# A fused attention and feed-forward kernel: the start planned on given landing times, V of batch 1 loaded last, stores later in their queue

## The chip, the cores and the metric

The kernel runs on one core of one Trainium2 chip. The time is the device time of one execution in microseconds (us). The engines are named as in the profile: PE (TensorE, matrix multiplication), PEld (its weight loads), DVE (VectorE), ACT (ScalarE), POOL (GpSimd) and SP (SyncE, which here only issues DMAs).

## The reference

Attention over a window of 64 positions for 8 batches, 8 heads, 576 positions and a head size of 64, then a feed-forward layer with a hard-swish on the 4608 x 512 result:

```
scores = q @ k.T / sqrt(64), kept where 0 <= i - j < 64
attn   = softmax(scores);  x = attn @ v          # x: 4608 x 512
h = x @ w_in                                     # 4608 x 2048
out = (h * clip(h + 3, 0, 6) / 6) @ w_out        # 4608 x 512
```

All inputs and the output are float32. The kernel computes in bfloat16 with float32 sums.

## The kernel before, in words

**Tiles.** The feed-forward layer runs over nine tiles `t` of 512 tokens. A tile has a first part of 16 groups `fc` of four 512-column matmuls with `win` (line L600), whose results pass through ACT (L613) and DVE (L618) into `gT`, and a second part of 64 matmuls with `wout` (L637) into four output blocks `u`, each copied to `osb` (L648) and stored by SP. A batch has 576 tokens, so a tile holds the rows of one or two batches; attention of batch `t + 1` is worked into tile `t`. Attention goes by pairs of heads `g` (0 to 3). The last 64 positions of all pairs form one extra item, "e".

**Attention of a pair.** `scores` (L444) multiplies 64-row blocks of K and Q, ACT takes the exponential (L460). For batch 0 a mask called `far` is added by two matmuls beforehand (L437); later batches multiply by `mask` on DVE (L469). The product with V has two forms. `pv` (L541) gives the transposed result and, through columns of ones in `V`, the sums; ACT takes their logarithm and an exponential (L547, L550) and DVE multiplies (L561) into `xT`. `pv_rows` (L489) gives rows and sums in one, DVE divides (L499, L500), and `turn_x` (L515) transposes the result on PE, to be copied to `xT` (L297). Batch 0's pairs take the second form, all others the first.

**How Q and K come in transposed.** For batches 0 and 1 POOL loads them with a cast into `Aq` and `Ak`, and PE transposes them by `fold_pair` (18 small matmuls, L409; copied out at L414). From batch 2 on SP loads float32 rows into a `stage` buffer, POOL casts them to `nq` and `nk` (L297), and SP transposes by DMA (`turn`, L320), first Q, then K. V is always loaded by SP into a stage and cast into `V` (`cast_v`, L297).

**What sets the order.** Each operation is added to a `Plan` with its engine, an estimated duration, what it reads and writes, a priority and sometimes operations that it must follow. `settle` runs through the plan with estimated times eight times and emits all instructions in the order of their planned start. So a number in the plan issues nothing itself, but it moves instructions on every engine's queue, and the engines run their queues in order. A DMA's planned end comes from `landing`, a model of the two DMA queues (SP's and POOL's). POOL's DMAs and some of its other work are tied in a chain by `then`: in batch 0's stage q and k of pairs 1 to 3, the masks, `touch` (a one-column copy that reads a loaded buffer, so that what follows waits for that load; before, it reads V of pair 2), the four parts of `win`, the first two of `wout`, q and k of batch 1, the last two of `wout`, and `hold`. `hold` writes into the stage buffer of batch 1's V, so V's loads on SP wait for it. Before, it is a memset; the plan lists `wout` part 2 as what it reads, but the instruction itself reads nothing.

**Filling matmuls.** Ahead of the first tile `warm` (L805) puts matmuls with `ident` into planned gaps of PE, sized by the gap.

Of the kernel before, what the change touches and what calls it, by code (L numbers as in the profile page):

```python
# [10 lines left out]
F32 = mybir.dt.float32  # L11
# [10 lines left out]
WINDOW = 64  # L22
FAR = 8.0e9


class Op:
    def __init__(self, eng, dur, emit, reads, writes, prio, stream):
# [9 lines left out]
        self.packets = self.cost = 0  # L37
# [4 lines left out]
class Plan:  # L42
# [4 lines left out]
    LAT = 150  # L47
    NSLOT = {"n": 2, "b": 1, "a": 2}
# [37 lines left out]
    def landing(self, begin, packets, cost, other):  # L86
        now, left = begin, packets
        for a, b, c in other:
# [6 lines left out]
            per = 0.9 * (cost + c) / 16  # L95
# [6 lines left out]
    def solve(self, rank, seen):  # L102
# [4 lines left out]
        free = {}  # L107
# [8 lines left out]
        while left:  # L116
            best = None
            for key, lst in streams.items():
                cands = lst[:1] if key in inorder else lst[:24]
                for op in cands:  # L120
# [51 lines left out]
            if op.packets:  # L172
# [3 lines left out]
                op.done = ring[eng] + 700  # L176
# [12 lines left out]
def kernel(  # L189
# [9 lines left out]
    nc = tc.nc  # L199
# [58 lines left out]
    HEAD = 2  # L258
    LATE = 13
# [55 lines left out]
    def dma(packets, cost, out_ap, in_ap, reads=(), writes=(), stream="ld", after=(), kind="copy", eng="SP"):  # L315
# [5 lines left out]
        op = add(eng, 760 if eng == "POOL" else 480, em, reads=reads, writes=writes,  # L321
# [14 lines left out]
    def load_pair(n, src, b, g, i, x):  # L336
        st = stage[i][:, x * R * D : (x + 1) * R * D]
        dma(P, 106, st, src[b, 2 * g : 2 * g + 2].rearrange("h (p j) d -> (h p) (j d)", j=R), writes=[("stp", n)])
        copy_op(R * D, A[n][:, g, :, :].rearrange("p j d -> p (j d)"), st, ("ACT", "DVE"),
                [("stp", n)], [("A", n, g)] + st_keys(i, 0, NG, range(KB)), sbuf=True, prio=700)  # L340
# [6 lines left out]
    def load_tok(src, b, i, g0, g1, kbs=tuple(range(KB))):  # L347
        st = stage[i][:].rearrange("p (k h d) -> p k h d", k=KB, h=H)
        hs = slice(2 * g0, 2 * g1)
        for kb in kbs:  # L350
# [3 lines left out]
                writes=[("st", i, g, kb) for g in range(g0, g1)])  # L354

    def st_keys(i, g0, g1, kbs):
        return [("st", i, g, kb) for g in range(g0, g1) for kb in kbs]
# [17 lines left out]
    def v_keys(g):  # L375
        return ["V1"] + [("V", g, x) for x in (0, NE + 1, NE + 2)]
# [21 lines left out]
    def fold_pair(n, g, b, gate, kinds=("n", "b", "a")):  # L398
# [3 lines left out]
        op = pe(R * 30, None, [("A", n, g), "fold"], [key], "pick", alloc=(name,), kinds=kinds, after=gate, mode="r")  # L402
# [19 lines left out]
    def scores(b, items, gate, stream="att", pr=300, masked=False, kinds=("a",)):  # L422
# [5 lines left out]
        op = pe(sum(2 * (NG if e else NM) * 14 for e in ends) + (2 * mm(MAIN) if masked else 0), None,  # L428
# [49 lines left out]
    def pv_rows(b, g, i, after, stream="att", pr=300):  # L478
# [4 lines left out]
        op = pe(2 * NM * 17, None, [("pT", i)] + v_keys(g), [key], stream, alloc=(name,), kinds=("a", "b"), after=after, mode="c")  # L483
# [208 lines left out]
    scrap = sb([P, 1], F32, "scrap")  # L692

    def touch(i, g, kb, after=()):

        st = stage[i][:].rearrange("p (k h d) -> p k h d", k=KB, h=H)
        return add("POOL", 100, lambda: nc.gpsimd.tensor_copy(out=scrap[:], in_=st[:, kb, 2 * g, 0:1]),
# [150 lines left out]
```

## Time and profile before

| | before |
|---|---|
| runs shown, us | 310.7, 311.97, 313.28; median 311.97 |
| profiled execution, us | 310.29, span 308.6 |
| granted TensorE clock | 1.000 |
| PE busy | 296.0 us (96%) |
| PEld / DVE / ACT / POOL busy | 51% / 63% / 69% / 28% |
| moved by DMA | 48.18 MB, 156 GB/s over the span |

The page gives the busy time of each engine, the chain of work that ended last, and the groups of instructions. A row of the timeline has the start, the time, the engine, the line, the operation with `out<-in` and the count of instructions merged, and in brackets the idle time of the engine before it and what ended it. SPq is SP's queue of DMA issues. In an answer on DMAs, the last number of an issue's row is the median time from issue to landing.

### The profile page before, as it was taken

The page shows a single profiled execution, that of the slowest core. Times are in us where ns is not written, and L with a number is a line of the kernel's source. Part 1 is how long each engine was busy: PE and PEld are TensorE (multiplying, and loading weights), DVE is VectorE, ACT ScalarE, POOL GpSimd, SP SyncE. Part 2 cuts the span into 40 slices and gives each one's busy share as a digit, 9 for nine tenths or more (in the row PEclk, how much of TensorE's full clock was granted, in tenths as well). Part 3 has the DMA queues.
Part 4 walks back from the last instruction along what each step waited for, and adds up shares of the span by engine and source line. Part 5 has one row for each costly group of instructions (what it writes and reads, how often), then busy time and mean ns, then how long its engine had stood idle before and what let it go on. Part 6 is the DMA issues. An engine that isn't in the chain of part 4 may idle for free.

```text
span 308.6 us, 6865 instructions
## 1 busy us (share of the span) xinstructions
PE 296.0 (96%) x2777; PEld 157.2 (51%) x2777; DVE 193.0 (63%) x292; ACT 213.2 (69%) x332; POOL 87.0 (28%) x82
## 2 busy tenths in 40 slices
PE   4989999899899999999999999999999999999995
PEld 3774455443554455445588654455445544444442
DVE  4366767876497758476857685797577757206700
ACT  3748967785697878687868795879587957217611
POOL 7683003333643345433445000683400000000000
PEclk9999999999999999999999999999999999999999
DMA  8999995999999999999999999939100110010011
GB/s 184 170 205 192 199 212 161 225 213 241 214 221 209 259 208 185 235 278 202 203 177 224 244 208 211 240 20 220 71 0 12 58 71 0 34 71 34 0 68 68
DMA packets 136703, 48.18 MB, mean 156 GB/s; under 512 B 125920, under 2 KB 131808, under 8 KB 136672
## 3 DMA queue, kind: packets, MB, share of 16 engines
q1 hardware_dynamic: 130496, 41.50, 64.3%
q0 software_dynamic: 6176, 6.26, 12.4%
q8 instruction: 21, 0.34, 0.5%
q14 instruction: 10, 0.08, 0.1%
HBM read 36.70 MB, written 9.44 MB: 150 GB/s over the span
## 4 chain that ended last, share of the span: by engine, by line
PE 72%; issue 2%; DMA 2%; DVE 1%; ACT 1%
PE pn L637 34%; PE pn L600 13%; PE pa L600 10%; PE pb L600 8%; PE pa L541 3%; DMA Tk<-nk 2%; PE pa L444 2%; DVE xT L561 1%; PE pb L541 1%; PE pb L444 1%; ACT rec L547 0%; ACT osb L648 0%; ACT rec L550 0%
## 5 line engine op out<-in xcount | busy, mean ns | idle before, releaser
L637 PE MATMUL pn<-wout,gT 128*128 128x512 bf16 x576 | 132.1, 379 | 0.1
L600 PEld LDWEIGHTS <-win 128*128 128x128 bf16 x640 | 61.9, 98 | 62.0 <-issue 2.0
L637 PEld LDWEIGHTS <-gT 128*128 128x128 bf16 x576 | 53.7, 98 | 59.5 <-issue 0.4
L600 PE MATMUL pn<-xT,win 128*128 128x512 bf16 (+1 forms) x284 | 65.0, 358 | 0.0
L297 POOL CAST V<-stage 64x2048 bf16<-64x2048 f32 (+2 forms) x22 | 39.2, 1784 | 52.1 <-DMA stage<-in_v_dram 22.8
L613 ACT ACTIVATE t<-pn,half 128x512 bf16<-128x512 f32 x64 | 44.1, 689 | 8.9 <-PE pn L600 7.6
L600 PE MATMUL pa<-xT,win 128*128 128x512 bf16 (+1 forms) x208 | 48.6, 358 | 1.2 <-DVE xT L561 1.2
L618 DVE SCALAR_TENSOR_TENSOR gT<-t,pn 128x512 bf16<-128x512 bf16 x64 | 43.9, 686 | 9.3 <-ACT t L613 9.0
L618 DVE SCALAR_TENSOR_TENSOR gT<-t,pa 128x512 bf16<-128x512 bf16 x47 | 32.2, 687 | 22.8 <-ACT t L613 22.5
L561 DVE TENSOR_TENSOR xT<-pa,rec 64x512 bf16<-64x512 f32 (+1 forms) x52 | 34.8, 668 | 12.5 <-ACT rec L550 11.5
L613 ACT ACTIVATE t<-pa,half 128x512 bf16<-128x512 f32 x47 | 32.2, 686 | 9.7 <-PE pa L600 9.2
L648 ACT COPY osb<-pn 128x512 f32<-128x512 f32 x23 | 13.4, 582 | 35.7 <-PE pn L637 35.7
L618 DVE SCALAR_TENSOR_TENSOR gT<-t,pb 128x512 bf16<-128x512 bf16 x33 | 22.6, 686 | 23.5 <-ACT t L613 23.5
L600 PE MATMUL pb<-xT,win 128*128 128x512 bf16 (+1 forms) x148 | 34.8, 356 | 0.0
L547 ACT ACTIVATE rec<-pa 64x512 f32<-64x512 f32 (+1 forms) x52 | 29.9, 575 | 2.9 <-PE pa L541 1.0
L297 POOL CAST nq<-stage 128x2048 bf16<-128x2048 f32 (+1 forms) x12 | 15.6, 1319 | 56.3 <-DMA Tq<-nq 28.3
L613 ACT ACTIVATE t<-pb,half 128x512 bf16<-128x512 f32 x33 | 22.8, 690 | 8.5 <-PE pb L600 8.5
L460 ACT ACTIVATE pT<-pa 128x1024 bf16<-128x1024 f32 x25 | 24.5, 1021 | 5.4 <-PE pa L444 5.4
L469 DVE TENSOR_TENSOR pT<-pT,mask 128x1024 bf16<-128x1024 bf16 x28 | 22.1, 809 | 8.0 <-ACT pT L460 7.9
L541 PEld LDWEIGHTS <-V 128*128 128x128 bf16 x512 | 18.8, 98 | 6.9 <-DVE xT L561 0.7
L550 ACT ACTIVATE rec<-rec 128x512 f32<-128x512 f32 (+1 forms) x36 | 20.8, 577 | 0.7
L297 POOL CAST nk<-stage 128x2048 bf16<-128x2048 f32 (+1 forms) x12 | 14.9, 1267 | 14.9 <-DMA stage<-in_k_dram 14.0
(80 smaller groups left out, 174.6 us busy)
## 6 DMA issues: line engine op xcount, KB each, us to landing
out_dram<-osb SPq DMA_DIRECT2D x36, 256.0 KB, 2.4
stage<-in_q_dram SPq DMA_DIRECT2D x24, 256.0 KB, 4.7
stage<-in_k_dram SPq DMA_DIRECT2D x24, 256.0 KB, 5.2
stage<-in_v_dram SPq DMA_DIRECT2D x24, 256.0 KB, 5.2
stage<-in_v_dram SPq DMA_DIRECT2D x22, 128.0 KB, 6.2
win<-in_moe_w_in_dram POOLq DMA_DIRECT2D x4, 512.0 KB, 8.4
wout<-in_moe_w_out_dram POOLq DMA_DIRECT2D x4, 512.0 KB, 16.8
stage<-in_q_dram SPq DMA_DIRECT2D x6, 128.0 KB, 4.8
```

What stands on the lines that cost most here:

```text
L297: alts = {e: (cost[e], (lambda e=e: cpy(e)(out=out_ap, in_=src())), sbuf) for e in engines}
L460: nc.scalar.activation(out=p_[:].rearrange("p j h c -> p h j c"), in_=wide(op, name)[:, :, 0 : n * D].rearrange("p h (j c) -> p h j c", c= ...
L469: nc.vector.tensor_tensor(out=pp, in0=pp, in1=mask[:, m0 : m0 + n, :, :].rearrange("p j h c -> p (j h c)"), op=MULT)
L541: nc.tensor.matmul(wide(op, name)[:, h, y * D : (y + 1) * D], lhsT=V[:, blk, g, h * D : h * D + P], rhs=p_[:, y, h, :], start=True, stop=True)
L547: add("ACT", act(n), lambda h=h: nc.scalar.activation(out=rc[rows[h], 0:n], in_=wide(op, name)[rows[1 - h], h, 0:n], func=LN), reads=[key] ...
L550: add("ACT", act(n), lambda: nc.scalar.activation(out=rc[:, 0:n], in_=rc[:, 0:n], func=EXP, scale=-1.0), writes=[("rc", ri, 0), ("rc", ri, ...
L561: nc.vector.tensor_tensor(out=o, in0=a, in1=z, op=MULT)
L600: nc.tensor.matmul(bank(op, name)[:, to : to + n], lhsT=win16[:, g, fc * P : (fc + 1) * P], rhs=xT[:, g, o : o + n], start=(g == 0), stop= ...
L613: nc.scalar.activation(out=t1[ti][:], in_=bank(op, name), func=RELU, bias=half[:], scale=1.0 / 6.0)
L618: nc.vector.scalar_tensor_tensor(out=gT[:, fc, :], in0=t1[ti][:], scalar=1.0, in1=bank(op, name), op0=MIN, op1=MULT)
L637: nc.tensor.matmul(bank(op, name), lhsT=gT[:, fc, col : col + P], rhs=wout16[:, fc, :], start=(fc == 0), stop=(fc == NFC - 1))
L648: alts = {e: (f(DM), (lambda e=e: cpy(e)(out=osb[oi][:], in_=bank(op, name))), False) for e, f in (("DVE", dve), ("ACT", act))}
```

## The change

In the plan: the first 18 loads get landing times from a table, stores may not be planned earlier than 3 us after their result is ready, a DMA transpose is planned with 4.6 us of SP's time, and some costs differ. In the program:

- Batch 0: q and k of pair 2 are issued ahead of the masks and those of pair 3 behind them; `mask` (used from the end item of batch 0 on) is built later. `touch` reads `Aq` of pair 3, so `win` waits for that load. V of pairs 2 and 3 is cast pair by pair.
- Of the columns of ones in `V`, DVE writes the two that batch 0's pairs need, and POOL the rest, ahead of `hold`.
- `wout` and batch 1 by turns: two parts, q and k of pairs 0 and 1, two parts, q and k of pairs 2 and 3. `hold` is a copy that reads the last part of `wout`.
- Batch 1's pairs 1, 2 and 3 take `pv_rows` and `turn_x`.
- Filling matmuls have 256 columns instead of 128 and fill 0.6 of a gap instead of 0.8.

In the order that comes of it, PE takes the scores of batch 2's pairs 0 and 1 ahead of the first 12 matmuls of `wout` of the second tile instead of behind them; on SP the ten loads of batch 1's V stand without a store between them, two stores stand between the transposes of batch 2 where a store, two loads of V and one of q stood, and the last two loads of batch 2's V stand behind both transposes.

```diff
+LANDED = {
+    "SP": (2950, 3650, 6000, 6700, 7500, 8300, 11100, 11600, 12100, 13200, 13500, 13700),
+    "POOL": (4500, 6300, 7800, 9000, 10000, 10900),
+}
...
+    LAG = 3000
...
-            per = 0.9 * (cost + c) / 16
+            per = (1.1 if 79 in (cost, c) else 0.9) * (cost + c) / 16
...
+                            if op.stream == "st":
+                                t = max(t, d.done + self.LAG)
...
-                op.done = ring[eng] + 700
+                op.done = max(op.land or ring[eng] + 600, t + dur)
+                ring[eng] = max(ring[eng], op.done - 600)
...
+    HOLD = 3
+    ROWS = (1, 2, 3)
...
-        op = add(eng, 760 if eng == "POOL" else 480, em, reads=reads, writes=writes,
+        op = add(eng, 740 if eng == "POOL" else 4600 if kind == "turn" else 500, em, reads=reads, writes=writes,
...
-    def attend(b, first, second, stream="att"):
+    def attend(b, first, second, stream="att", rows=()):
...
-            pv(b, x, i, (), stream)
+            if x in rows:
+                _, *og = pv_rows(b, x, i, (), stream)
+                turn_x(b, x, *og, stream, kinds=("b", "a"))
+            else:
+                pv(b, x, i, (), stream)
...
-    def touch(i, g, kb, after=()):
+    def touch(n, g, after=()):
...
+        return add("POOL", 200, lambda: nc.gpsimd.tensor_copy(out=scrap[:], in_=A[n][:, g, 0, 0:1]),
+                   reads=[("A", n, g)], writes=["scrap"], after=after, prio=2000)
...
-    def hold(i, reads, after=()):
+    def hold(i, part, after=()):
...
-        return add("POOL", 80, lambda: nc.gpsimd.memset(stage[i][:, 0:1], 0.0), reads=reads,
-                   writes=st_keys(i, 0, NG, range(KB)), after=after)
+        return add("POOL", 200, lambda: nc.gpsimd.tensor_copy(out=stage[i][:, 0:1], in_=wout16[:, 4 * part + 3, 0:1]),
+                   reads=[("wout", part)], writes=st_keys(i, 0, NG, range(KB)), after=after)
...
+    then(load_cast("q", q, 0, 2, 3, after=chain))
+    then(load_cast("k", k, 0, 2, 3, after=chain))
+    then(add("POOL", 1050, mask_pool, writes=["m32"], after=chain))
+    then(add("POOL", 900, far_pool, reads=["m32"], writes=["far"], after=chain))
+    then(load_cast("q", q, 0, 3, 4, after=chain))
+    then(load_cast("k", k, 0, 3, 4, after=chain))
...
-    first = cast_v(iv, 0, 2, (THREE,) * 3, prio=700)
-    then(touch(iv, 2, 0, chain))
+    cast_v(iv, 0, 2, (("POOL", "DVE"),) * 3, prio=700)
+    then(touch("q", NG - 1, chain))
...
     for g in range(0, NG, 2):
+        for i in range(2):
+            then(load_wout(g + i, after=chain))
+        if g == 0:
+            then(add("POOL", 1300, mask_pool16, reads=["m32"], writes=["mask"], after=chain))
         then(load_cast("q", q, 1, g, g + 2, after=chain))
         then(load_cast("k", k, 1, g, g + 2, after=chain))
-    for i in range(2, 4):
-        then(load_wout(i, after=chain))
...
-    then(hold(iv, [("wout", 2)], chain))
+    then(add("POOL", 1900, lambda: nc.gpsimd.memset(V[:, :, :, D + 2 : 2 * D], 1.0), writes=["V2"], after=chain))
+    then(hold(iv, HOLD, chain))
...
-    rank = {("PE", "att"): 300, ("PE", "pick"): 300, ("POOL", "issue"): 300, ("SP", "turn"): 1000, ("SP", "st"): 500}
+    rank = {("PE", "att"): 300, ("PE", "pick"): 300, ("POOL", "issue"): 0, ("SP", "turn"): 1000, ("SP", "st"): 500}
```

More of the change, by code (lines that the diff above doesn't have):

```diff
@@ L36, in __init__ @@
         self.got = {}
-        self.packets = self.cost = 0
+        self.packets = self.cost = self.land = 0
         self.home = eng
@@ L811 @@
                 if at is not None and at < COLD:
-                    for _ in range(int((op.start - at) * 0.8 / mm(P))):
+                    for _ in range(int((op.start - at) * 0.6 / mm(2 * P))):
                         warm(op)
```

67 lines of the change are left out of this document (33 added, 34 removed).

## The prediction

> **What bounds the kernel now.** I read the page first, then the busy time by windows, then the timeline of the first 97 us, then the DMA answers of single windows.
>
> ```profile
> span 308.6 us, 6865 instructions
> ...
> PE 296.0 (96%) x2777; PEld 157.2 (51%) x2777; DVE 193.0 (63%) x292; ACT 213.2 (69%) x332; POOL 87.0 (28%) x82
> ...
> 120.00:150.00 30.00, 30.00 (x254) 14.83 (x253) 20.50 (x32) 23.00 (x38) 10.57 (x7) 1.00 1.15 224
> ...
> 119.47 5.18 PE pn L637 x24
> ```
>
> The second number of a window row is the TensorE busy time, the third from the end the granted clock, full here. Between 120 and 150 us, in the third and fourth tile, TensorE is busy in every microsecond, and the row of the chain gives 5.18/24 = 0.216 us for one 512-column matmul; nothing in this change makes that cheaper. All that can be won lies before about 95 us: in the start, and in the waits of the first two tiles. The timeline of the start (start, duration, engine, line, operation, idle time before it):
>
> ```profile
> 4.36 0.69 POOL L318 DMA_DIRECT2D Aq<-in_q_dram  x1
> 5.68 0.69 PE L409 MATMUL pn<-fold,Aq 64*64 64x64 bf16 x18
> 6.69 0.89 POOL L683 TENSOR_SCALAR far<-mask 128x64 bf16<-128x64 f32 x2
> 8.89 2.72 SPq L318 DMA_DIRECT2D stage<-in_v_dram  x1
> 8.98 0.47 PE L409 MATMUL pa<-fold,Aq 64*64 64x64 bf16 x18
> 11.32 1.02 ACT L460 ACTIVATE pT<-pb 128x1024 bf16<-128x1024 f32 x1 [0.24 <-PE pb L444]
> 12.94 1.54 POOL L318 DMA_DIRECT2D win<-in_moe_w_in_dram  x2 [0.28 <-issue]
> 13.55 0.76 DVE L414 COPY Tq<-pn 128x576 bf16<-128x576 bf16 x1 [4.63 <-PE pn L409]
> 14.20 2.12 ACT L297 CAST V<-stage 64x1024 bf16<-64x1024 f32 x2
> 16.18 0.45 PE L489 MATMUL pb<-V,pT 128*64 128x65 bf16 x16
> 17.30 1.59 POOL L318 DMA_DIRECT2D wout<-in_moe_w_out_dram  x2
> 18.88 0.71 POOL L318 DMA_DIRECT2D Aq<-in_q_dram  x1
> 20.45 0.22 PE L489 MATMUL pa<-V,pT 128*64 128x65 bf16 x2 [1.18 <-issue]
> 22.62 0.39 PE L515 MATMUL pa<-ident,opg 128*128 128x128 bf16 x4
> 22.84 0.81 PE L600 MATMUL pb<-xT,win 128*128 128x512 bf16 x3
> ```
>
> The main loop starts at 22.84. VectorE stands idle for 4.63 us ahead of the copy at 13.55, and only then casts V; ScalarE casts its part at 14.20, behind the exponentials that began at 11.32. So the first product with V comes at 16.18. The last one loses 1.18 us to "issue", a wait that no semaphore explains. The next two views are DMA answers (windows of one issue, 16 to 28 us, 33 to 44 us; the last number of an issue row is the time to landing) and the timeline up to the second tile:
>
> ```profile
> Aq<-in_q_dram POOLq DMA_DIRECT2D x1, 144.0 KB, 6.4
> ...
> stage<-in_v_dram SPq DMA_DIRECT2D x1, 64.0 KB, 5.6
> ...
> win<-in_moe_w_in_dram POOLq DMA_DIRECT2D x1, 512.0 KB, 5.6
> ...
> wout<-in_moe_w_out_dram POOLq DMA_DIRECT2D x1, 512.0 KB, 12.2
> ...
> Aq<-in_q_dram POOLq DMA_DIRECT2D x1, 288.0 KB, 15.8
> ...
> DMA packets 2455, 2.47 MB, mean 206 GB/s; under 512 B 74, under 2 KB 2453, under 8 KB 2453
> ...
> q0 software_dynamic: 1675, 1.73, 92.0%
> q1 hardware_dynamic: 1650, 0.41, 28.4%
> ```
>
> ```profile
> 29.22 17.30 SPq L318 DMA_DIRECT2D stage<-in_v_dram  x9
> 35.59 0.76 PE L409 MATMUL pa<-fold,Aq 64*64 64x64 bf16 x36
> 48.54 0.36 SPq L318 DMA_DIRECT2D out_dram<-osb  x1
> 49.60 0.62 SPq L318 DMA_DIRECT2D stage<-in_q_dram  x1
> 58.46 0.59 PE L600 MATMUL pa<-xT,win 128*128 128x512 bf16 x2
> 61.12 0.38 PE L600 MATMUL pa<-xT,win 128*128 128x512 bf16 x1 [0.40 <-DVE xT L561]
> 64.63 4.70 SPq L320 DMA_TRANSPOSE Tq<-nq  x1
> 71.94 4.25 SPq L320 DMA_TRANSPOSE Tk<-nk  x1
> 74.17 5.80 POOL L297 CAST V<-stage 128x2048 bf16<-128x2048 f32 x3 [7.91 <-PE pn L600]
> 78.26 0.64 PE L444 MATMUL pa<-Tq,Tk 64*128 64x64 bf16 x32 [1.87 <-DMA Tk<-nk]
> 83.09 0.63 PE L541 MATMUL pb<-pT,V 128*128 128x64 bf16 x16
> 94.58 0.38 PE L600 MATMUL pa<-xT,win 128*128 128x512 bf16 x1 [0.16 <-DVE xT L561]
> ...
> DMA to landing us min/median/max: 4.9/5.3/6.3
> ```
>
> Three stalls of TensorE are to be seen. At the second tile six matmuls should take 1.3 us, yet the seventh starts 2.66 us after the first: 1.4 lost to the normalised rows of batch 1. The scores of batch 2 wait 1.87 us for the transpose of K. The third tile waits 0.16.
>
> **The change, part by part.** The new costs and landing times of the planner issue nothing; they act through the order of each engine's instructions, which is what I cost here. *Release of W_in.* Before, the release stood behind V and the issue came at 12.94. Now it stands behind the q of pair 3. That load was issued at 4.36 and landed 6.4 later, at 10.8. But the two masks, whose last instruction ends at 7.58 (6.69 + 0.89), now come ahead of it: about 2.0 us of GpSimd work, so it is issued at 6.4. If the software queue is still full, it lands at 10.8 all the same; with an empty queue it takes what the W_in part took, 5.6, and lands at 12.0. I take 11.1, nearer to the full queue, and 0.5 for touch and issue: W_in at 11.6, 1.3 us earlier (bounds 0.5 and 1.6). Four issues in a row instead of two and two change nothing, since the DMA engines had no gap.
>
> *Start.* The far mask is ready 1.2 us earlier and V's first half is cast before the exponentials, so products of V no longer wait at 16.18. The bound is then the last piece of V: issued at 8.89, landed at 14.5. Behind it ScalarE casts three half pieces (half of 2.12/2 each, 1.6), takes the last exponential (1.02), and the last product follows at 17.4. From the last product to the main loop it took 22.84 − 20.45 = 2.4; VectorE now serves two products close together, so 2.8. Main loop at 20.2, gain 2.6. Best: 3.4 (nothing queues); worst: 1.4 (the 1.18 us of "issue" comes back). Part of it is taken by the next wait: the fold at 35.59 needs the batch-1 q issued at 18.88, landed 15.8 later, at 34.7; with W_in 1.3 earlier that is 33.4, and the fold would come at 33.0. So 2.2 remain.
>
> "Runtime: NRT & Kernel Launch" of the Trainium skill (section Instruction fetch mechanics) says that instructions come in blocks of 256 and that crossing a block is mostly hidden. The 1.18 us with no releaser would be an exception; by the rule the start gains its full 3.4, by the row 1.4.
>
> *Rows of batch 1.* For pairs 1 to 3 the product goes through rows (0.45 by the row at 16.18, and a transposition of 0.39 as at 22.62) in place of 0.63: 0.2 each, 0.6 more on TensorE, of which I take 0.5 as the ends overlap. In return two logarithms and an exponential per pair fall away from ScalarE, and the 1.4 us at the second tile goes (bounds 0.7 to 1.4).
>
> *W_out, batch 1, V last.* The old hold is a memset that reads nothing of W_out: V of batch 1 was issued from 29.22, in the midst of W_out, and nine issues took 17.3 us. Between 33 and 44 us both queues moved as many packets (1675 and 1650), but V only 0.41 MB of it, against 206 GB/s for the software queue alone. The new hold copies from the last part of W_out, so it truly waits for that landing. In its way stand W_in, the whole of W_out and half of batch 1: 8 x 0.524 + 2 x 0.295 = 4.78 MB, 23.2 us at 206 GB/s. A W_in part of 0.524 MB (2.5 us) landed 5.6 after its issue, so 3.1 is added; the third 0.524 MB more, W_out's first, landed at 17.30 + 12.2 = 29.5, where this sum gives 28.7, so 0.8 to 1.7 more by the end of W_out. Hold: 11.6 + 3.1 + 23.2 + 1.2 = 39.1 (bounds 37.8 and 40.7). Behind it on GpSimd's queue are the casts of V of batch 1; on SP's queue, behind V's first load, everything else. Most of V's columns of ones are now written by GpSimd ahead of the hold. The trace has no such memset; far's two instructions take 0.89 for 512 columns, so 1984 take between nothing and 3.4, and the wait for the hold hides it all. Without that wait it would come on top.
>
> V's ten issues at 0.62 take 6.2, so q of batch 2 is issued at 45.4 instead of 49.60: 4.2 earlier, mostly because no store (48.54) stands in the queue for a result.
>
> *Stores later.* From q of batch 2 to the transpose of Q there are 15 DMAs before as after, 15.0 us (64.63 − 49.60). Q's transpose goes at 60.4 and holds the queue 4.7; two stores take 1.0; K's goes at 66.1 and lands 4.9 to 6.3 later, 72.0. The scores that need it now stand ahead of 12 matmuls of W_out (2.6 us) which before lay ahead of them. TensorE could come to them at 58.46 − 2.2 + 0.5 + 64 x 0.216 = 70.6, so 1.4 us of waiting stays. Next is V of batch 2: its last two loads now stand behind K's transpose (66.1 + 4.25 = 70.4), land some 4 later (bounds 2.5 to 5.2) and take 5.8 to cast: 80.2. TensorE reaches the first product at 72.0 + (83.09 − 78.26) + 2.6 = 79.4, so it waits 0.8 more. Before, that product began at 83.09 with the same matmuls done: 2.9 gained. With the 0.16 of the third tile, 3.1; 3.3 if the last loads come 0.2 sooner in the emptied queue, which I take.
>
> **Sum.** The profiled execution took 310.29 (span 308.6 and 1.7 around it), so 307.0; the median of the runs shown, 311.97, is 1.7 above it, and the same gain gives 308.7. The likeliest case alone: 307.6 to 309.8. One per cent, 3.1 us, is about what a measurement of this kernel can tell from no change.
>
> **Rivals.** *All in time (0.17).* If the hold ends at 38.5 or before and V's last loads land in 2.5, both transfers of batch 2 are there and TensorE sets the time: 2.2 − 0.5 + 1.4 + 1.87 + 0.16 = 5.1, so 306.8. For it speaks the sum without its surplus, 37.9; against it that W_out's first part already landed 0.8 behind the sum.
>
> *The release comes no earlier (0.18).* The order is built on landing times of a queue in which pair 3 was issued at 4.36. At 12.0 for its q, W_in goes at 12.5, and everything behind the hold 0.9 later; with the products of V of batch 1 then waiting 0.5: gain 1.9, 310.1.
>
> *The hold costs more than it brings (0.12).* The software queue moved 1.73 MB in the 11 us from 33 to 44, 157 GB/s. At that pace to the end the hold is at 46.4, 7.3 later, V, q and K of batch 1 and 2 with it: 4.0 slower, 316.0. From a hold at 42.4 nothing is gained; from 45.5 it is over 1% slower. Against it: at that time the other queue was at work, which now stands still.
>
> *A colder clock (0.05).* Fewer filling matmuls stand in the start (28 of 256 columns for 97 of 128). The folds took 0.69 at 5.68 and 0.47 at 8.98: the array speeds up once it has been busy. Were it to fall back, the main loop would run slow for about as long again, 3.3 us (8.98 − 5.68), and lose at most half of that, 1.7; the 1.4 us in which TensorE would wait for K anyway hide most of it: 309.0. The Trainium skill's "TensorE: Matmul & The Clock Gate" (Part 1: The HAM clock gate) has a rule for this, half the clock after an idle window of some 3.4 us; no stretch without a matmul is that long in the timeline of the start after its first fold, so the trace gives the rule no hold here.
>
> **How the numbers follow.** The likeliest case has 0.48; rather more than half of it lies below 308.9, which with the first rival makes 0.45 for faster. Same: the rest of it, the late release and the clock, 0.41. Slower: the hold, and 0.02 for what I haven't seen, 0.14. The range must reach from the best start with all in time to a hold a few us late: 305.6 to 312.8.
>
> **What would show it.** Right: W_in issued near 11.6; main loop near 20; the first V load of batch 1 near 39 and its ten issues in about 6 us; no gap at the second tile; K's transpose of batch 2 issued near 66. Wrong: a hold after 42, folds of batch 1 waiting for their loads, or a start later than 21.5.

## The result, and the profile after

| | before | after |
|---|---|---|
| median of the runs, us | 312.29 (310.7 to 313.28, 4 runs) | 307.3 (307.19 to 308.54, 4 runs) |
| profiled execution, us | 310.29, span 308.6 | 307.36, span 305.6 |
| granted TensorE clock | 1.000 | 0.999 |

The ratio of the medians is 0.985 (95% interval 0.980 to 0.990): faster by 1.5%. The medians differ by 5.0, the profiled executions by only 2.9, because the other runs of the kernel before lie up to 3.0 above its profiled one; the traces can explain the 2.9. The first lines of the page after:

```profile
span 305.6 us, 6684 instructions
...
PE 290.8 (95%) x2674; PEld 153.0 (50%) x2720; DVE 192.1 (63%) x293; ACT 209.1 (68%) x325; POOL 91.4 (30%) x86
```

The timeline of the start after (start, duration, engine, line, operation, idle time before it). The lines of the code have moved: `fold_pair` is L427, `scores` L462, `pv` L559, `pv_rows` L507, W_in's matmuls L618, W_out's L655, the casts L307, SP's loads L328 and transposes L330.

```profile
6.52 0.56 POOL L328 DMA_DIRECT2D Aq<-in_q_dram  x1
11.84 0.19 POOL L718 COPY scrap<-Aq 128x1 bf16<-128x1 bf16 x1 [0.35 <-DMA Aq<-in_q_dram]
12.30 2.98 POOL L328 DMA_DIRECT2D win<-in_moe_w_in_dram  x4 [0.27 <-issue]
13.85 0.45 PE L507 MATMUL pb<-V,pT 128*64 128x65 bf16 x16
19.53 0.59 PE L618 MATMUL pb<-xT,win 128*128 128x512 bf16 x2
```

W_in is issued at 12.30 (12.94 before), the first product with V comes at 13.85 (16.18), and the main loop begins at 19.53 (22.84): 3.3 earlier. The timelines of PE, POOL and SP up to the third tile, put in order of time:

```profile
28.46 1.76 POOL L777 MEMSET V<- 128x1984 bf16 x1
...
33.45 0.76 PE L427 MATMUL pa<-fold,Aq 64*64 64x64 bf16 x36 [1.04 <-DMA Aq<-in_q_dram]
...
40.01 0.21 POOL L723 CAST stage<-wout 128x1 f32<-128x1 bf16 x1 [9.79 <-DMA wout<-in_moe_w_out_dram]
40.24 5.73 SPq L328 DMA_DIRECT2D stage<-in_v_dram  x10
46.02 2.57 SPq L328 DMA_DIRECT2D stage<-in_q_dram  x3
48.69 1.32 SPq L328 DMA_DIRECT2D out_dram<-osb  x1
52.62 0.35 PE L559 MATMUL pa<-p,V 128*128 128x64 bf16 x6 [0.89 <-POOL V L307]
57.67 0.81 PE L618 MATMUL pb<-xT,win 128*128 128x512 bf16 x3
58.96 0.38 PE L618 MATMUL pb<-xT,win 128*128 128x512 bf16 x1
61.18 4.20 SPq L330 DMA_TRANSPOSE Tq<-nq  x1
66.56 3.46 SPq L330 DMA_TRANSPOSE Tk<-nk  x1
71.86 0.64 PE L462 MATMUL pa<-Tq,Tk 64*128 64x64 bf16 x32 [0.21 <-DMA Tk<-nk]
74.09 6.22 POOL L307 CAST V<-stage 128x2048 bf16<-128x2048 f32 x3 [10.64 <-DVE pT L487]
80.37 0.58 PE L559 MATMUL pb<-pT,V 128*128 128x64 bf16 x14 [0.86 <-POOL V L307]
90.50 0.81 PE L618 MATMUL pa<-xT,win 128*128 128x512 bf16 x3
91.79 0.38 PE L618 MATMUL pa<-xT,win 128*128 128x512 bf16 x1
```

The 3.3 us of the start have shrunk to 2.1 at the fold (33.45 for 35.59). The second tile has no gap: its seventh matmul follows the first by 1.29. SP issues the ten loads of V in a row as soon as the hold lets go, at 40.24; K's transpose of batch 2 goes at 66.56 (71.94), the scores that need it come at 71.86 (78.26), the first product with V of batch 2 at 80.37 (83.09), and the third tile's seventh matmul at 91.79 (94.58), 2.8 ahead. From there to the end both take the same time to within 0.2, so this is the gain.

The DMA answers on the window from 12 to 72 us, first before, then after (tenths of busy time in slices of 1.5 us):

```profile
DMA  8399999999999999999999961686999999999998
```

```profile
DMA  7799999999999999999887979999999999999997
```

Before, the DMA engines lose most of the slice from 13.5 to 15 us, and some 3.4 us between 46.5 and 54 (slices of 6, 1, 6, 8 and 6). After, no slice lies below 7.

### The profile page after: what moved, and what is told of

The parts are those of the page before. It is cut to its first block, busy times and chain, and to the rows that moved or that the text cites. A ratio compares the mean times of both kernels' runs of the same rounds, so it can differ in the third digit from the quotient of the medians.

```text
span 305.6 us, 6684 instructions
## 1 busy us (share of the span) xinstructions
PE 290.8 (95%) x2674; PEld 153.0 (50%) x2720; DVE 192.1 (63%) x293; ACT 209.1 (68%) x325; POOL 91.4 (30%) x86
## 4 chain that ended last, share of the span: by engine, by line
PE 78%; DMA 11%; POOL 4%; issue 2%; ACT 2%; DVE 1%; SPq 1%; DVEq 0%; ACTq 0%; POOLq 0%
PE pn L655 36%; PE pn L618 14%; PE pa L618 11%; PE pb L618 8%; DMA wout<-in_moe_w_out_dram 6%; PE pa L559 4%; PE pa L462 2%; DMA Tk<-nk 2%; DMA Aq<-in_q_dram 2%; POOL V L307 1%; DMA stage<-in_v_dram 1%; DMA stage<-in_q_dram 1%; PE pb L559 1%; SPq L328 1%; POOL Ak L328 1%
## 5 line engine op out<-in xcount | busy, mean ns | idle before, releaser
L655 PE MATMUL pn<-wout,gT 128*128 128x512 bf16 x548 | 128.0, 379 | 2.2 <-issue 1.1
L618 PEld LDWEIGHTS <-win 128*128 128x128 bf16 x640 | 61.8, 98 | 60.3
L655 PEld LDWEIGHTS <-gT 128*128 128x128 bf16 x576 | 53.6, 98 | 59.2
L618 PE MATMUL pn<-xT,win 128*128 128x512 bf16 (+1 forms) x280 | 64.3, 358 | 0.2
L307 POOL CAST V<-stage 64x2048 bf16<-64x2048 f32 (+5 forms) x25 | 41.9, 1677 | 65.2 <-PE pa L559 32.1
L618 PE MATMUL pa<-xT,win 128*128 128x512 bf16 (+1 forms) x199 | 47.2, 358 | 0.3
L636 DVE SCALAR_TENSOR_TENSOR gT<-t,pa 128x512 bf16<-128x512 bf16 x46 | 31.5, 687 | 22.3 <-ACT t L631 22.0
L579 DVE TENSOR_TENSOR xT<-pa,rec 64x512 bf16<-64x512 f32 (+1 forms) x50 | 33.4, 668 | 11.5 <-ACT rec L568 10.5
L618 PE MATMUL pb<-xT,win 128*128 128x512 bf16 (+1 forms) x147 | 35.0, 356 | 0.6 <-issue 0.5
L565 ACT ACTIVATE rec<-pa 64x512 f32<-64x512 f32 (+1 forms) x50 | 28.8, 575 | 3.7 <-PE pa L559 1.8
L487 DVE TENSOR_TENSOR pT<-pT,mask 128x1024 bf16<-128x1024 bf16 x28 | 23.7, 864 | 3.0 <-ACT pT L478 2.9
L307 POOL CAST nq<-stage 128x2048 bf16<-128x2048 f32 (+1 forms) x12 | 15.6, 1331 | 27.0 <-issue 15.0
L559 PEld LDWEIGHTS <-V 128*128 128x128 bf16 x464 | 17.0, 98 | 9.0 <-POOL V L307 2.0
L307 POOL CAST nk<-stage 128x2048 bf16<-128x2048 f32 (+1 forms) x12 | 14.9, 1269 | 16.7 <-DMA stage<-in_k_dram 16.1
L568 ACT ACTIVATE rec<-rec 128x512 f32<-128x512 f32 (+1 forms) x33 | 18.9, 573 | 0.6
```

What stands on the lines that cost most here:

```text
L307: alts = {e: (cost[e], (lambda e=e: cpy(e)(out=out_ap, in_=src())), sbuf) for e in engines}
L487: nc.vector.tensor_tensor(out=pp, in0=pp, in1=mask[:, m0 : m0 + n, :, :].rearrange("p j h c -> p (j h c)"), op=MULT)
L559: nc.tensor.matmul(wide(op, name)[:, h, y * D : (y + 1) * D], lhsT=V[:, blk, g, h * D : h * D + P], rhs=p_[:, y, h, :], start=True, stop=True)
L565: add("ACT", act(n), lambda h=h: nc.scalar.activation(out=rc[rows[h], 0:n], in_=wide(op, name)[rows[1 - h], h, 0:n], func=LN), reads=[key] ...
L568: add("ACT", act(n), lambda: nc.scalar.activation(out=rc[:, 0:n], in_=rc[:, 0:n], func=EXP, scale=-1.0), writes=[("rc", ri, 0), ("rc", ri, ...
L579: nc.vector.tensor_tensor(out=o, in0=a, in1=z, op=MULT)
```

## The experiments

Theory A was that a chain of transfers (W_in, W_out, batch 1, hold, V of batch 1, batch 2 with its transposes, the casts of its V on GpSimd) sets the pace up to the third tile. The main rival, B, was that the earlier start alone brings the gain. Single parts have rivals of their own, named where they are tested. In the table, the third tile is the start of its first matmul in the profiled execution, the loop that of the first tile. From there to the end most of the new kernels take 215.1 us (the kernel before 215.6); e4 takes 0.9 more, e7 0.5, e8 0.8, e9 0.3 and e12 2.2. The runs were made on four chips (e1 to e4, e5 to e8, e9 to e11, e12), and each ratio compares with the kernel before on the same chip, so medians from different groups are not set side by side.

| kernel | median (lowest to highest), us | ratio to before (95%) | span | loop | third tile |
|---|---|---|---|---|---|
| kernel before | 312.29 (310.7 to 313.28) | 1 | 308.6 | 22.8 | 93.0 |
| changed kernel | 307.3 (307.19 to 308.54) | 0.985 (0.980 to 0.990) | 305.6 | 19.5 | 90.5 |
| the same, once more (e11) | 307.7 (307.37 to 308.0) | 0.986 (0.981 to 0.990) | 306.0 | 20.1 | 90.9 |
| e1 old hold | 308.81 (308.19 to 310.75) | 0.988 (0.981 to 0.996) | 307.3 | 20.1 | 92.2 |
| e2 stores early | 308.41 (308.21 to 309.75) | 0.987 (0.980 to 0.994) | 306.9 | 19.8 | 91.8 |
| e3 no rows | 310.56 (308.41 to 312.11) | 0.993 (0.989 to 0.997) | 310.3 | 19.7 | 95.2 |
| e4 start only | 313.81 (311.97 to 316.29) | 1.003 (0.998 to 1.007) | 310.4 | 19.7 | 94.3 |
| e5 more bytes | 310.38 (309.15 to 312.16) | 0.995 (0.992 to 0.998) | 308.6 | 19.5 | 93.5 |
| e6 less bytes | 307.51 (306.73 to 308.16) | 0.986 (0.983 to 0.990) | 305.0 | 19.3 | 89.9 |
| e7 casts shared | 307.69 (307.12 to 308.29) | 0.987 (0.983 to 0.992) | 306.1 | 19.6 | 90.4 |
| e8 transposes first | 308.33 (307.45 to 309.3) | 0.989 (0.985 to 0.994) | 305.7 | 21.4 | 89.9 |
| e9 loop late | 309.69 (308.7 to 310.37) | 0.993 (0.990 to 0.996) | 308.1 | 23.0 | 92.7 |
| e10 stores last | 306.97 (306.45 to 307.47) | 0.983 (0.979 to 0.987) | 305.6 | 20.6 | 90.4 |
| e12 transposes, then V | 307.7 (307.14 to 308.87) | 0.988 (0.983 to 0.992) | 306.0 | 19.4 | 88.7 |

The changed kernel run again shows how far a single profile may be trusted: in ten runs its span went from 305.5 to 306.8. Differences under half a microsecond between two profiles are not read below.

**e1: the old hold.**

```diff
-    ... nc.gpsimd.tensor_copy(out=stage[i][:, 0:1], in_=wout16[:, 4 * part + 3, 0:1]),
+    ... nc.gpsimd.memset(stage[i][:, 0:1], 0.0),
```

> The changed kernel with one instruction altered: the hold on GpSimd is again a memset that reads nothing, so V of batch 1 is issued amid W_out, from about 30.5 in place of 40.24; the order on every engine stays. Theory A (the end of the gain is set by the chain of transfers W_in, W_out, batch 1, hold, V, batch 2): V takes a share of the engines away from W_out and batch 1, q and k of pairs 2 and 3 land some 4 later than 41.35 and 42.79, the folds at 41.76 and 43.41 wait for them; span 305.6 + 1.5 to 4 = 307.1 to 309.6. Theory B (the start alone brings the gain): the span stays at 305.6, within 0.5.

The span became 307.3, 1.7 more. From the timelines of SP and PE of this kernel:

```profile
30.57 15.38 SPq L328 DMA_DIRECT2D stage<-in_v_dram  x10
43.30 0.47 PE L427 MATMUL pb<-fold,Aq 64*64 64x64 bf16 x18 [1.64 <-DMA Aq<-in_q_dram]
67.17 3.53 SPq L330 DMA_TRANSPOSE Tk<-nk  x1
86.78 0.64 PE L559 MATMUL pb<-pT,V 128*128 128x64 bf16 x16 [0.77 <-DVE xT L579]
```

Ten issues take 15.38 instead of 5.73, and TensorE falls back where A put it, at the fold of q of pairs 2 and 3: 1.5 later (43.30 for 41.76). Their q and k land 1.9 and 2.4 later, not 4, and K's transpose is only 0.6 later. So of the 1.5 only 0.9 is left at the first product with V of batch 2, where TensorE had waited anyway; the rest of the 1.7 is lost again at 86.78, in a wait of 0.77 for VectorE that neither theory had. V last hardly brings V earlier, since the same bytes have to pass; it brings batch 1's q and k earlier.

**e2: stores early.**

```diff
-    LAG = 3000
+    LAG = 0
```

> The changed kernel without the 3 us that the planner adds before a store. TensorE and ScalarE keep their order; on SP's queue the first store moves in front of the last three V loads of batch 1, the second behind two loads of q, the third in front of Q's transpose of batch 2; one V cast goes from GpSimd to VectorE. Theory A: the hold keeps V back until 40.2, by which time the first result is there (copied 43.5 to 44.1), so no store blocks the queue; one DMA more ahead of Q's transpose is 0.6, K's transpose is issued at about the same 66.6: span 305.6 to 306.0. Theory C (later stores are what frees the queue): stores block as in the kernel before, q of batch 2 is issued 2 to 4 later than 46.02, span 307 to 308.6.

306.9, 1.3 more: between the two. From the timelines of SP and PE:

```profile
44.09 0.46 SPq L328 DMA_DIRECT2D out_dram<-osb  x1
63.01 4.19 SPq L330 DMA_TRANSPOSE Tq<-nq  x1
73.07 0.64 PE L462 MATMUL pa<-Tq,Tk 64*128 64x64 bf16 x32 [1.85 <-DMA Tk<-nk]
```

```profile
DMA  8599999999999999999997977999996899999999
```

A was right that no store blocks the queue (the first goes 0.1 behind the load before it) and wrong on the price: Q's transpose goes 1.8 later, not 0.6. The DMA more in front accounts for 1.0 of it (q goes at 47.02 for 46.02). The other 0.8 arises between q and the transpose: one issue of k takes 2.84 there, and the DMA engines have a gap from 57 to 60 us (the slices 6 and 8). Why SP was held there no run shows. In the kernel after, the 13 loads and 2 stores from 46.02 to 61.18 take a microsecond each, though SP can issue a DMA in some 0.5 us; the DMA engines are full through this stretch, so they are the likely brake. And the stores run beside the loads there. What that does to the rate can be read from the windows, first of the kernel after, then of e10 below, which issues no store in this window (the last number is GB/s):

```profile
52.00:62.00 10.00, 9.33 (x82) 4.82 (x84) 5.10 (x10) 6.05 (x11) 4.01 (x4) 1.00 1.14 227
```

```profile
52.00:62.00 10.00, 9.61 (x84) 4.93 (x85) 5.52 (x12) 6.09 (x12) 3.91 (x4) 1.00 1.15 203
```

With stores among the loads the engines move 227 GB/s (230 in e11), with loads alone 203. So a store put early stands in front of V's loads, and is missing later, where it would have cost little.

**e3: no rows in batch 1.**

```diff
-    ROWS = (1, 2, 3)
+    ROWS = ()
```

> The changed kernel with pairs 1 to 3 of batch 1 normalised by logarithms again. Theory A: the gap of 1.4 at the second tile comes back, TensorE has 0.5 less to do, so it reaches the scores of batch 2 0.9 later; but there it waits for K's transpose (0.6 in all) and then for the V casts (0.86), so 0 to 0.3 is left: span 305.6 to 305.9, and the wait at the first product of V of batch 2 is nearly gone. Theory D (the rows shorten the path itself): span 306.5.

Both theories fell short: the best of ten runs has a span of 306.7, the profiled one 310.3. From its timeline of PE, and from its busy time by windows of a microsecond (second number PE, third from the end the granted clock):

```profile
58.32 0.38 PE L618 MATMUL pb<-xT,win 128*128 128x512 bf16 x1 [1.77 <-DVE xT L579]
72.74 0.64 PE L462 MATMUL pa<-Tq,Tk 64*128 64x64 bf16 x32 [1.18 <-DMA Tk<-nk]
81.99 0.58 PE L559 MATMUL pb<-pT,V 128*128 128x64 bf16 x14 [2.47 <-POOL V L307]
```

```profile
84.00:85.00 1.00, 0.89 (x3) 0.33 (x3) 0.03 (x1) 0.98 (x3) 0.78 (x2) 0.50 1.08 204
```

The gap at the second tile is back (1.77, and 0.40 behind it). TensorE reaches the scores of batch 2 at 71.56, about as in the kernel after (71.65) and not 0.9 later as A had it, because the planner put four matmuls of W_in behind them. In all, 84 matmuls of the two layers stand ahead of the first product with V instead of 92, so TensorE waits 2.47 there with 1.7 us of work left over (8 x 0.216) that the kernel after does before. In this execution K and V also come 0.9 and 1.6 later, and the long wait is followed by some 3.3 us at half the clock, which costs up to 1.7 more. Why the chain is later here (V's issues 0.7 slower, its last landing 0.7 longer) is not settled; it may be the spread between executions. What stands is that at least 1.1 is lost without rows and with the order that comes of it, not 0 to 0.3; what rows alone are worth is not shown.

**e4: the start only.** The orders of W_out and batch 1, the hold, the rows, the stores' 3 us and the planned cost of a transpose go back.

```diff
-    LAG = 3000
+    LAG = 0
-    ROWS = (1, 2, 3)
+    ROWS = ()
...
+    for i in range(2):
+        then(load_wout(i, after=chain))
...
+    for i in range(2, 4):
+        then(load_wout(i, after=chain))
```

> The changed kernel with only the new order of batch 0 (and the release of W_in) kept: the old hold, W_out 0 and 1, batch 1, W_out 2 and 3 in this order, no rows in batch 1, stores not delayed, the old cost of a transpose. The loop starts near 19.5 as in the changed kernel. Theory A: the transfers behind W_in are only 0.6 earlier than in the kernel before, so most of the 3.3 of the start is given back in waits at the folds of batch 1, at K and at V of batch 2: span 308.6 less 0.5 to 1.2 = 307.4 to 308.1. Theory B (the start alone brings the gain): span 305.6 to 306.1.

310.4, and in the medians no gain at all (1.003). B is out in the form that the start alone brings the gain whatever the order behind it: the loop begins at 19.7, and the third tile at 94.3, behind the 93.0 of the kernel before. A had the direction, but expected 307.4 to 308.1. From the view of what SP waited for (38 to 72 us), the DMA answer on 12 to 72 us, the timeline of PE and the windows:

```profile
SPq L328 <- DVE osb L666: 12.0, 1, 12.0
```

```profile
DMA  9899999999999999999995048869999978999996
```

```profile
60.87 2.72 PE L618 MATMUL pn<-xT,win 128*128 128x512 bf16 x6 [3.70 <-DVE xT L579]
```

```profile
62.00:63.00 1.00, 1.00 (x4) 0.35 (x3) 0.24 (x1) 0.00 (x0) 0.00 (x0) 0.50 0.97 227
```

Here stores stand between V's loads again. One waits 12.0 us for its result, and SP's queue with it; when W_out is through, the DMA engines stand idle (the slices 5, 0 and 4 from 43.5 to 48). V of batch 1 comes late, the second tile waits 3.70, and half the clock follows. This is not the kernel before with an earlier start, either: there the first store stands behind V's ninth load, here behind the fifth, and the start alone on the old order of SP's queue was not run. And since several edits go back at once, e4 doesn't tell what each of them costs; e1, e2 and e3 do that singly.

**e5 and e6: more and fewer bytes in the chain**, with the same order of instructions on every engine.

```diff
+            op.emit = lambda: (nc.gpsimd.dma_start(out=spare[:], in_=moe_w_out[0 : 4 * P, :]...), one())     # e5, part 0
```
```diff
+        if i == 3:
+            op.emit = lambda: None                                                                           # e6
```

> The changed kernel with one transfer more: the first part of W_out (0.524 MB) is also loaded into a tile that nobody reads, ahead of W_out on GpSimd's queue. The order on every engine stays, the start isn't touched. Theory A (chain of transfers): everything behind it comes 2.5 later (0.524 MB at 206 GB/s): first fold of batch 1 at 35.9 for 33.45, hold at 42.5 for 40.01, K of batch 2 lands at 74.3; span 305.6 + 2.5 = 308.1 (1.9 to 2.8). Theory B (the start sets it): span 305.6, within 0.4.

> The changed kernel with one transfer less: the last part of W_out is not loaded, its matmuls read the third part instead (so the output is not the reference's), and the hold waits for the third part. The order on every engine stays. Theory A: the hold comes 2.6 earlier, at 37.4, and so do V of batch 1 and all of SP's queue behind it; TensorE can use no more of it than it waits now: 0.89 at the end product of batch 1, 0.6 at K and 0.86 at V of batch 2, less where its own work comes next: span 305.6 less 1.0 to 1.6 = 304.0 to 304.6. Theory B: no change, 305.6 within 0.3.

With more bytes, from the timelines of SP and PE (lines moved by 7):

```profile
33.22 0.41 PE L566 MATMUL pb<-p,V 128*128 128x64 bf16 x8 [2.84 <-POOL V L784]
42.78 6.43 SPq L328 DMA_DIRECT2D stage<-in_v_dram  x10
```

V's first load is 2.54 later, as computed (0.524 MB at 206 GB/s), and the span 3.0 longer, slightly over A's bounds: what is added to the chain here comes back whole in the time. TensorE first falls back at 33.22, in a wait for the columns of ones in V, and 2.5 of it is left at the fold (35.98 for 33.45). With fewer bytes (lines moved by 3):

```profile
37.54 6.41 SPq L328 DMA_DIRECT2D stage<-in_v_dram  x10
50.66 0.40 PE L536 MATMUL pb<-ident,opg 128*128 128x128 bf16 x4 [1.28 <-DVE opg L521]
```

V's first load is 2.7 earlier, and only 0.6 is gained in the profile, nothing in the median. TensorE now waits 1.28 for VectorE, which divides the rows of batch 1. The chain binds, with TensorE close behind it: A, but with less to be had than expected.

**e7 and e8: the waits of the second tile taken away.** In e7 one of the three V casts of batch 2 goes to ScalarE; e8 puts both transposes ahead of V's loads as well.

```diff
-                cast_v(iv, 0, NG, (("POOL",),) * 3)
+                cast_v(iv, 0, NG, (THREE,) * 3 if b == 2 else (("POOL",),) * 3)
...
+            tk = (turn("q"), turn("k"))                       # e8
+        load_tok(v, b, iv, 0, NG, after=tk)                   # e8
```

> The changed kernel with the three V casts of batch 2 (only of this batch) open to GpSimd, ScalarE and VectorE; the planner gives one of the two half-partition casts to ScalarE, between exponentials. Theory A: GpSimd's casts end near 78.3 in place of 80.3, the first product of V no longer waits 0.86: span 304.7 to 305.0, if ScalarE's 2 us between the exponentials delays none of them past the end product. Theory E (the wait is only moved to the exponentials or to the next tile): span 305.4 to 306.

> The kernel with shared V casts of batch 2, and with both transposes of batch 2 ahead of all its V loads on SP's queue: Q's transpose is issued at about 57.9 for 61.18, K's at about 63.5 (when k is cast) for 66.56. Theory A: K lands near 68.8 for 71.81, so TensorE doesn't wait for it (0.6 gained); the V loads land as late as now, about 74, the casts end by 78; with the 0.86 at V the span is 305.6 less 1.2 to 1.6 = 304.0 to 304.4. Theory E: V's loads, all five behind K's transpose, become the next wait and the gain stays under 0.6: 305.0 or more.

Neither is faster. In e7 the first product comes at 78.89 for 80.37, but with eight matmuls of W_out (1.7 us) fewer ahead of it, so TensorE is no further; the third tile begins at 90.44, and 0.5 is lost in the sixth tile, 0.4 of it in a wait for K's transpose: theory E. In e8's profile the first loads landed late (q of pair 1 at 7.13 for 5.41), and the loop began 1.9 later than in the kernel after (21.40). The third tile begins 0.65 earlier all the same (89.85); 0.8 is then lost in it, most of it (0.58) in a wait for VectorE. Here, as in e10 and e12, the planner also put the scores of batch 2 ahead of the last eight matmuls of W_in; what that does alone was not run.

**e9: the loop late.** All transfers and the release stay, 15 matmuls more delay the loop.

```diff
+                for _ in range(15):
+                    nc.tensor.matmul(bank(op, op.alloc[0]), lhsT=ident[:], rhs=ident[:]..., start=True, stop=True)
```

> The changed kernel with 15 filling matmuls of 512 columns more (15 x 0.216 = 3.24 us) on TensorE just ahead of the main loop, which then starts as late as in the kernel before; the order of all else, the release of W_in and all transfers stay. Theory A (the chain of transfers sets the pace up to the third tile): the 3.24 go into the waits that TensorE has on the way, 1.04 at the fold, 0.89 at the end product, 0.6 at K, 0.86 at V; results come up to 2.2 later, and the second store on SP's queue waits for its own by that, so the chain itself may move by 0 to 1: span 305.6 + 0.3 to 1.3 = 305.9 to 306.9. Theory B (the start sets it): 305.6 + 2.5 to 3.2 = 308.1 to 308.8.

Its median is 309.69, 2.0 above the changed kernel on the same chip; its span of 308.1 is 2.1 above. Neither theory: 1.1 to 1.2 of the 3.24 vanish in waits, the rest stays. From the timelines of SP and PE, and behind them a row of ScalarE's:

```profile
39.84 6.74 SPq L328 DMA_DIRECT2D stage<-in_v_dram  x10
46.62 3.81 SPq L328 DMA_DIRECT2D stage<-in_q_dram  x3
50.52 0.97 SPq L328 DMA_DIRECT2D out_dram<-osb  x1
68.60 3.47 SPq L330 DMA_TRANSPOSE Tk<-nk  x1
82.53 0.58 PE L559 MATMUL pb<-pT,V 128*128 128x64 bf16 x14 [1.01 <-POOL V L307]
```

```profile
46.25 0.59 ACT L666 COPY osb<-pn 128x512 f32<-128x512 f32 x1 [0.61 <-PE pn L655]
```

The chain itself has moved: the hold came at 39.62, even a little earlier than the 40.01 of the kernel after, but the first store goes at 50.52 for 48.69, and K's transpose 2.0 later. The store did not wait for its result, which ScalarE had copied by 46.8; SP's queue came to it only then. V's ten issues took 6.74 for 5.73 and q's three 3.81 for 2.57, one issue of each far longer than the rest (1.62 and 2.53), and between 42 and 43.5 us the DMA engines moved only 97 GB/s. Why, and whether the late loop has a part in it, no run shows. TensorE came to the first product with V at 81.52 and waited 1.01 for casts of V that were late by the queue; without that it would have been about 1.1 behind the kernel after instead of 2.1, which is within A's bounds. So B's 2.5 did not come, and A's size can't be told apart from this queue. Without the early start the other edits are worth 0.5 by the profiles (308.6 to 308.1) and 0.7% by the medians; the start without them is worth nothing (e4); together they bring 2.6 to 3.0, or 1.5%.

**e10, e11 and e12: stores last, and transposes before V.** In e10 the four stores of the first tile may go only behind all loads of batch 2; in e12 V's loads of batch 2 stand behind both transposes as well. e11 is the changed kernel itself.

```diff
+        st.no_sooner = 66500 if u < 4 else 0
...
+                                t = max(t, d.done + self.LAG, op.no_sooner)
...
+        load_tok(v, b, iv, 0, NG, after=tk)                   # e12
```

> The changed kernel with the four stores of the first tile held back behind both transposes and all loads of V of batch 2. Two stores less ahead of Q's transpose, four less ahead of K's. Theory A (each DMA in the queue ahead of the transposes costs about 0.5 to 1, as the run with early stores showed): K's transpose is issued at 62 to 64 for 66.56 (k must be cast first), lands at 67 to 69, V's last load lands by 72; TensorE waits neither at K nor at V, but as with less bytes ahead of the hold only part of it stays: span 305.6 less 0.5 to 1.0 = 304.6 to 305.1. Theory F (the stores ahead cost nothing, since the queue waits for the cast of k anyway): 305.6 within 0.3.

> The changed kernel once more, beside the two others on the same chip, for their comparison: median 307.3 and span 305.5, up to 1.3 above in single runs; granted clock 0.998 to 1.000 in each.

> The changed kernel with the four stores of the first tile and all five V loads of batch 2 behind both transposes of batch 2. Theory G (formed from the runs before: from 14 to 72 us the DMA engines move some 210 GB/s without a hole, so what counts is how many bytes stand ahead of a transpose, 0.26 MB or 1.2 us for each load or store): ahead of Q's transpose are four V loads less than in the run with the stores last, so it goes at 58 for 62.2; K's waits for the cast of k and goes at about 63.4 for 66.5, and lands at 68.5; V's loads land by 73, their casts on GpSimd end by 79; TensorE waits for neither by more than 0.3: the third tile starts at 89.3 to 89.8 for 90.43, median 0.6 to 1.1 below that run's 306.97: 305.9 to 306.4. Theory H (V takes over as the next wait, its casts end at 80 as in the changed kernel): 306.9 to 307.7.

e10 has the best median, 306.97 against 307.7 for e11 on the same chip; five of its six runs lie below all six of e11, though the intervals of the two ratios overlap. From its timelines of SP and PE:

```profile
62.20 4.14 SPq L330 DMA_TRANSPOSE Tq<-nq  x1
71.41 0.64 PE L462 MATMUL pa<-Tq,Tk 64*128 64x64 bf16 x32 [1.72 <-DMA Tk<-nk]
```

A's size is right, its way is not. Q's transpose is not earlier with two stores less ahead of it: without them the engines move 203 GB/s between 52 and 62 us (the row shown under e2), and one load of V has come in front. K's transpose is no earlier either (66.50 for 66.56), as F had it, but not for F's reason: the cast of k had ended at 63.32, and K's transpose followed Q's, which ended at 66.34. What went is the wait at V, 0.86 in the kernel after and 1.60 in e11: all but the last of V's loads now land early, and two of the three casts are done by 69.5. From e12's timelines:

```profile
62.48 3.09 SPq L330 DMA_TRANSPOSE Tk<-nk  x1
69.42 0.64 PE L462 MATMUL pa<-Tq,Tk 64*128 64x64 bf16 x32
88.67 0.81 PE L618 MATMUL pb<-xT,win 128*128 128x512 bf16 x3
107.59 0.58 PE L559 MATMUL pb<-pT,V 128*128 128x64 bf16 x14 [0.82 <-POOL V L307]
```

As G had it, taking four loads of V (1.05 MB) from in front of the transposes brings K's to 62.48, neither K nor V is waited for, and the third tile begins at 88.67, 1.8 before the kernel after. And all of it is given back one tile later: the third tile takes 33.4 instead of 31.2, with waits for V of batch 3 (0.82) and for its masked exponentials (0.93). The median of 307.7 is that of e11 on another chip (ratios 0.988 and 0.986). So G's mechanism held and its time did not.

## Why the prediction was right, point by point

- *Release of W_in.* Predicted 11.6 (bounds 11.3 to 12.4), measured 12.30. The load of q of pair 3 took 5.2 from 6.52, as with an emptied queue; the value taken was the wrong end of the bounds. The hold came 0.9 late (40.01 for 39.1), mostly by this. SP's queue made good 0.4 of it (K's transpose at 66.56 for 66.1), and K's landing, 5.3 us after its issue where 5.9 were taken, the rest: luck. The step also held that the DMA engines had no gap at the old release; the slice from 13.5 to 15 us before, at 3, is one, and in the kernel after it stands at 7.
- *Start.* Predicted 20.2 (best 19.4), measured 19.53; the 1.18 us of "issue" did not come back. The last product with V came at 17.60 (17.4), and from it to the loop took 1.9, not 2.8. By the Trainium skill's "Runtime: NRT & Kernel Launch" (Instruction fetch mechanics), the crossing of a block is mostly hidden, by which the start would gain its full 3.4. The trace agrees in the gain (3.3); whether the 1.18 us before was such a crossing no run shows.
- *Fold of batch 1.* q landed at 33.41, predicted 33.4; 2.1 remained, predicted 2.2. The number was right, the way half of it: W_in was issued 0.6 earlier, not 1.3, and from there to q's landing it took 21.1 instead of 21.8. Why it took less is open.
- *Rows.* The gap of 1.4 is gone. What rows alone are worth stays open: e3 loses at least 1.1 without them, for the prediction's net 0.9, but with another order on TensorE.
- *V's ones.* The memset takes 1.76, inside the bounds. But the step named the wrong cover: not only the hold stands behind it, the end product of batch 0 reads these columns too. In the kernel after that product starts at 30.28, just behind the memset's end; in e5 the memset comes later and TensorE waits 2.84 for it. Any more time on GpSimd would have shown as a wait, up to the 1.04 that the fold behind it waits anyway.
- *Ten V issues and 15 DMAs.* 5.73 for 6.2 and 15.16 for 15.0. The numbers were right, since they were taken from a row with the same bytes; the reason was half of it. In the kernel before, SP waited 1.9 for the result of the store at 48.54, so "no store stands in the queue for a result" accounts for 1.9 of the 3.6 us by which q of batch 2 goes earlier (46.02 for 49.60). And the 15 DMAs take a microsecond each because, as e10 and e12 show, the loads' bytes on full DMA engines set the pace.
- *K and V of batch 2.* K's transpose at 66.56 (66.1), its landing at 71.8 (72.0), the first product at 80.37 (80.2). Of the predicted 1.4 of waiting for K little is left, because TensorE came later: the end product of batch 1 waits 0.89 for V, which no step had. The new place of batch 2's scores on TensorE was not run alone. By the rows it sets little: with the 12 matmuls of W_out ahead of them, TensorE would come to the product at some 79.3 (an estimate: 79.51 less the 0.21 at K), still before the casts of V end at 80.31.
- *Rivals.* The release did come late, at 12.30 for the 12.5 of that rival, but K and V of batch 2 did not come later by it. The software queue did not stay slow once it had the engines for itself (hold at 40.01, not 46.4), and the clock stayed full.
- *Sum.* 307.0 predicted from the profiled execution, 307.36 measured; 2.9 gained for 3.3. For the median 308.7 was forecast and 307.3 measured, below the likeliest case's 307.6 to 309.8 and near the 306.8 of the first rival, whose condition (a hold at 38.5 or before) did not come about. That the median fell by 5.0 and not by 2.9 comes from the other runs of the kernel before, of which no profile was kept: luck, and no merit of the sum.

Two steps would have misled in a neighbouring case. The sum takes the pace of SP's queue as fixed once the hold and the order are; in e9 both are the same, yet the queue runs 2.0 late, and 1.0 of the 2.1 comes of it. And e6, e7 and e12 each bring a wait that takes the place of the one removed.

## What to carry to other kernels

When one queue feeds the next stages, look first for idle slices of the DMA engines, and for what the issuing queue waited for in them: a store that waits for its result holds every load behind it. Where the engines are full, the bytes of the loads set the time, and a load put last delays at first nothing but itself; in e12 its price came a tile later. And test a gain at the end of the next tile, not where it arises: two of the kernels here (e8 and e12) were 0.6 and 1.8 earlier at the third tile and not faster.

## What the runs showed of the hardware

The granted clock can fall after short idle times. In e3 TensorE has no matmul from 79.5 to 82.0, and from 83 to 86.3 the clock is 0.50; in e4 an idle time of 3.7 is followed by 0.50 to about 63.6. "TensorE: Matmul & The Clock Gate" of the Trainium skill (Part 1: The HAM clock gate) speaks of half the clock after an idle window of about 3.4 us that runs freely; the length of the slow stretch agrees, but 2.5 us without a matmul were enough here, so such a window need not be wholly idle. They are not always enough: in e5 TensorE has no matmul for 2.84 us (30.4 to 33.2), and the clock stays at 1.00. Where a wait of that length does bring the slow stretch, it costs up to about 1.7 us more, half of its 3.3. The kernel before may meet it too: over the four chips, 15 of its 54 compared runs have a mean clock of 0.995 or less and a median of 313.6, the other 39 one of 311.5, while the changed kernel has 0.998 or more in all ten runs, with a median of 307.6. Where the clock falls in those runs of the kernel before, no profile shows.
